# Reordering the front of a state-space and gated-FFN kernel: rate placement in portions, more result buffers, iotas before waiting loads

## The chip, the cores and the metric

The kernel runs on one core of a Trainium2 chip. A core has five engines that work side by side: TensorE (PE in the profile) multiplies matrices and writes to PSUM; VectorE (DVE) and ScalarE (ACT) do elementwise work; GpSimd (POOL) does elementwise work and issues DMAs; SyncE (SP) only issues DMAs here. Each engine takes its instructions in one fixed order, and waits for another engine by semaphores. The metric is the device time of one execution in microseconds, less is better, as the median of several runs.

## The reference

`x` is 2048 tokens of 576 channels. The output and the gradients with respect to twelve of the inputs are wanted:

```python
xn = layernorm(x)                                  # over the 576 channels
P = exp((dt * A)[:, :, None] * arange(2048))       # 576 channels, 128 states, complex
K = einsum("dn,dnl,dn->dl", C, P, dt * B).real     # a convolution kernel per channel
s = irfft(rfft(xn, 4096) * rfft(K, 4096))[:2048] + xn * Dskip
g = silu((silu(xn @ w1) * (xn @ w3)) @ w2)         # hidden width 4608
out = x + s * g
```

Matrices are bf16. The change concerns the absolute value of P, that is real exponentials exp(dt * A_re * l).

## The kernel before

The program is one long straight line of instructions in stages: a front (`prologue`, lines 314 to 486) of some 88 us; a middle stage that builds K and runs the hidden layer of the gated FFN at once (`ssm_forward`, `ffn_hidden`); the FFN's output; and a backward pass of over 1000 us.

**What the front makes.** The real exponentials are split: position l is written as a sum of a coarse and a fine part, so a channel needs 16 + 64 columns instead of 2048. For 36 chunks of 16 channels that makes 36 x 1280 columns of 128 states. `early_exps` (line 678) computes them in 45 pieces of 1024 columns, numbered 0 to 44 below. One piece takes: TensorE products of a chunk's rates (`LR_`, 80 rows: 16 channels in three bf16 parts, with gaps) with a selection matrix (`sel_base`, made from iotas), into a PSUM tile of which there are two (`e_ps`); one ScalarE exponential into an SBUF tile `E_k`, of which there are four; and one store of 256 KB from SyncE's queue to DRAM (`E_dram`). For pieces 0 to 30 each product is issued twice, with the same result (`(0, 0, 1, 1) if n < 31`, line 683).

**Placing the rates.** `place_rates` (line 656) moves the rates of some chunks from the layout of the input (channels on partitions) into the rows that the products above want. For eight chunks it issues 48 small products (128 rows, 32 columns of weights, 128 columns wide: three parts, eight chunks, two halves) into one PSUM tile `t_ps`, of which there are two, and then one VectorE copy to `LR_`. It is called for chunks 0 to 3, 4 to 11, 12 to 19, 20 to 27 and 28 to 35. A chunk has 1280 columns, so chunk c is first read by piece 1.25 c.

**The selection matrix.** `selector_values` (line 546) has GpSimd write four iotas; `selector_base` (line 566) has VectorE turn them into the two parts of `sel_base` in place: 1024 columns for the fine positions and 256 for the coarse ones.

**The layer norm.** `ln_load` loads the even token tiles and copies the odd ones to DRAM in turned order (`odd_copy`); `ln_load_odd` loads them from there on GpSimd's queue, so it waits for that copy to land. `ln_stats` (line 205) takes statistics of 16 tiles on VectorE, `ln_root` the root of the variances, `ln_scale` the scaled tiles `xn_bf`; `ln_turn` (line 240) turns them on TensorE, ten steps with a VectorE copy each into `xnT`; `ln_fold` (line 259) makes eight sums and differences of tiles on VectorE that the Fourier spectrum of xn reads.

**What sets the order.** A scheduler orders each engine's instructions by a priority that the kernel sets (`self.pre(us)`), as far as data and buffers allow. In the front the order is pinned further: `Chain` (line 77) queues every instruction that is called through it behind the one before, for VectorE (`self.V`), ScalarE (`self.S`), GpSimd (`self.G`); `in_order` (line 651) does so for TensorE's placing products, exponential products and turns; `Behind` queues a SyncE load behind a given store. Such an edge holds only between instructions of one engine, and orders their issue without a wait. The text of `prologue` is therefore the order of work: `run(n)` issues pieces until n have been issued.

Other parts that the prediction speaks of: `load_rates` loads C and B behind early stores; the eight products Wr, Wi (lines 411 to 415) run on GpSimd; `store3` stores phase rates from GpSimd; `phase_rows` (line 717) issues twelve small loads `lhs_t` on SyncE's queue; `build_selectors` and `dft_signs` are short VectorE work; `early_spectrum` (line 692) transforms xn on TensorE, with copies to `u_e` on VectorE and ScalarE; the first steps of the hidden layer run between those.

## Time and profile before

| | us |
|---|---|
| median of 3 runs | 1737.71 (1734.06 to 1741.98) |
| the profiled execution | 1742.17 |
| its span, first to last instruction | 1740.0 |
| TensorE busy in the span | 1621.5 (93%) |
| VectorE busy | 1406.1 (81%) |
| ScalarE busy | 914.6 (53%) |
| GpSimd busy | 439.2 (25%) |

The mean granted clock of TensorE was 0.978. The profile gives, for each instruction, its start within the span, its duration, its line and the tiles that it writes and reads (`out<-in`), and for idle time what ended it. Where instructions go through a `Chain` they all show line 87, and `Behind` shows line 99, so one tells them apart by their tiles. A window gives the busy time of each engine in a stretch of the span, the clock that TensorE was granted (1.00 is full), and the share of time in which the DMA engines were busy; that share can exceed 1 a little in short stretches.

### The profile page before, as it was taken

The page shows a single profiled execution, that of the slowest core. Times are in us where ns is not written, and L with a number is a line of the kernel's source. Part 1 is how long each engine was busy: PE and PEld are TensorE (multiplying, and loading weights), DVE is VectorE, ACT ScalarE, POOL GpSimd, SP SyncE. Part 2 cuts the span into 40 slices and gives each one's busy share as a digit, 9 for nine tenths or more (in the row PEclk, how much of TensorE's full clock was granted, in tenths as well). Part 3 has the DMA queues.
Part 4 walks back from the last instruction along what each step waited for, and adds up shares of the span by engine and source line. Part 5 has one row for each costly group of instructions (what it writes and reads, how often), then busy time and mean ns, then how long its engine had stood idle before and what let it go on. Part 6 is the DMA issues. An engine that isn't in the chain of part 4 may idle for free. (4 is left out here: it accounts for less than half of the span.)

```text
span 1740.0 us, 33185 instructions
## 1 busy us (share of the span) xinstructions
PE 1621.5 (93%) x12784; PEld 981.9 (56%) x12841; DVE 1406.1 (81%) x2170; ACT 914.6 (53%) x1674; POOL 439.2 (25%) x675
## 2 busy tenths in 40 slices
PE   7798999999997999989999999999999998999998
PEld 4453444444444777545555555655555576777776
DVE  6669899989891656687975999678989966899898
ACT  5667778886762112585765857574655502111111
POOL 7142333322232111012111111111121351122143
PEclk8899999999998999999999999999999999999999
DMA  6558999998789999649577684969999999999992
GB/s 204 211 209 310 306 332 322 314 312 265 246 264 190 248 218 205 206 119 276 148 222 207 190 233 142 243 173 249 208 244 224 239 235 237 224 204 212 235 203 50
DMA packets 622060, 394.87 MB, mean 227 GB/s; under 512 B 426798, under 2 KB 565678, under 8 KB 621902
## 3 DMA queue, kind: packets, MB, share of 16 engines
q1 hardware_dynamic: 560140, 252.69, 59.8%
q0 software_dynamic: 39968, 121.11, 22.4%
q10 hardware_dynamic: 21794, 18.95, 3.7%
q8 instruction: 100, 1.64, 0.4%
q14 instruction: 58, 0.48, 0.1%
HBM read 122.18 MB, written 182.13 MB: 175 GB/s over the span
## 5 line engine op out<-in xcount | busy, mean ns | idle before, releaser
L2018 PEld LDWEIGHTS <-acts 128*128 128x128 bf16 x2304 | 222.7, 98 | 63.1 <-DMA acts<-GG_dram 1.7
L1966 PE MATMUL pgw<-ggu,xn_bf 128*128 128x512 bf16 x1152 | 256.6, 382 | 0.1
L1501 DVE TENSOR_TENSOR pr_q<-et_ps,pz 128x1024 f32<-128x1024 f32 x144 | 176.1, 1223 | 27.8 <-PE et_ps L1495 18.6
L1966 PEld LDWEIGHTS <-xn_bf 128*128 128x128 bf16 x1152 | 112.3, 98 | 133.0 <-issue 4.2
L1123 PEld LDWEIGHTS <-xnT 128*128 128x128 bf16 x1152 | 107.4, 98 | 140.6 <-issue 36.7
L1505 DVE TENSOR_REDUCE S_b<-pr_q 128x64 f32<-128x1024 f32 x144 | 175.4, 1218 | 3.9
L1878 PE MATMUL ph<-w2T,goT 128*128 128x512 bf16 (+3 forms) x800 | 159.1, 367 | 9.7 <-ACT gw L1968 3.5
L1123 PE MATMUL pg<-wmB_w,xnT 128*128 128x512 bf16 x532 | 148.8, 381 | 8.1 <-issue 5.0
L1123 PE MATMUL pu<-wmB_w,xnT 128*128 128x512 bf16 x563 | 150.3, 380 | 1.5 <-ACT u_t L1143 0.6
L1944 PE MATMUL pgw<-go_o,h_n 128*128 128x288 bf16 x1152 | 150.0, 287 | 1.1 <-ACT gh L1896 0.8
L1944 PEld LDWEIGHTS <-h_n 128*128 128x128 bf16 x1152 | 111.3, 98 | 31.4 <-issue 1.0
L1138 ACT ACTIVATE s_t<-pg 128x512 bf16<-128x512 f32 x144 | 87.3, 606 | 76.2 <-PE pu L1132 33.7
L2018 PE MATMUL px<-wT_ggu,acts 128*128 128x288 bf16 x896 | 121.9, 288 | 0.9 <-DMA wT_ggu<-in_B_w_dram 0.9
L1486 ACT COPY gz<-gz 64x1024 bf16<-64x1024 bf16 x36 | 37.5, 1043 | 159.3 <-DMA gz<-gK_dram 151.6
L1878 PEld LDWEIGHTS <-goT 128*128 128x128 bf16 (+1 forms) x800 | 65.0, 99 | 94.5 <-issue 39.6
L2018 PE MATMUL px<-wA,acts 128*128 128x288 bf16 x832 | 109.8, 286 | 1.9 <-DMA acts<-GG_dram 1.4
L1949 POOL DMA_DIRECT2D out_dram<-gw x36 | 20.1, 560 | 333.6 <-ACT gw L1948 323.6
L1972 POOL DMA_DIRECT2D out_dram<-gw x72 | 51.2, 715 | 209.8 <-ACT gw L1968 182.1
L1152 POOL DMA_DIRECT2D G_dram<-g_t x72 | 51.2, 712 | 187.7 <-ACT g_t L1140 121.2
L779 ACT ACTIVATE cs_k<-et_ps 128x512 bf16<-128x512 int16 x180 | 92.6, 629 | 1.2 <-PE et_ps L777 1.1
L1143 ACT CAST u_t<-pu 128x512 bf16<-128x512 f32 x144 | 86.6, 601 | 11.6 <-PE pu L1123 9.4
L1838 DVE TENSOR_TENSOR ggu<-ggu,h_n 128x1024 bf16<-128x1024 bf16 x72 | 48.9, 686 | 43.8 <-ACT ggu L1850 43.7
(342 smaller groups left out, 3212.8 us busy)
## 6 DMA issues: line engine op xcount, KB each, us to landing
G_dram<-g_t POOLq DMA_DIRECT2D x72, 256.0 KB, 4.9
U_dram<-u_t POOLq DMA_DIRECT2D x72, 256.0 KB, 4.8
H_dram<-h_t SPq DMA_DIRECT2D x72, 256.0 KB
Q_dram<-q_k SPq DMA_DIRECT2D x36, 512.0 KB
ggu<-G_dram POOLq DMA_DIRECT2D x18, 1024.0 KB, 9.5
h_n<-U_dram POOLq DMA_DIRECT2D x18, 1024.0 KB, 9.2
GG_dram<-ggu SPq DMA_DIRECT2D x36, 512.0 KB
GU_dram<-ggu SPq DMA_DIRECT2D x36, 512.0 KB
```

Source lines behind the costliest of these rows:

```text
L779: self.sin_last = nc.scalar.activation(out=CS[:, :, o:o + 256], in_=pt[:].bitcast(I16)[:, :, 0::2], func=ACT.Sin, scale=6.283184 / 2 ** 16)
L1123: ins = nc.tensor.matmul(pt[:], lhsT=xnT[:, c, ts], rhs=wm[w][:, c, :], start=(q == 0 and c == 0), stop=(q == 1 and c == nfull - 1))
L1138: nc.scalar.activation(out=s_t[:, :, q, :], in_=pgv, func=ACT.Silu)
L1143: nc.scalar.copy(out=u_t[:, :, q, :], in_=puv)
L1152: self.u_stores[step] = nc.gpsimd.dma_start(out=dst[fb * ng:(fb + 1) * ng, i0 // 4, :, i0 % 4:i0 % 4 + NT, :].rearrange("g p t f -> p g (t ...
L1501: nc.vector.tensor_tensor(out=pr[:], in0=T[z][:].rearrange("p s k d f j -> p (s k) (d f j)")[:, None] .to_broadcast([P, 2, 4, 4 * AV]), in ...
L1505: nc.vector.tensor_reduce(out=self.sums_of[-1][:, :, :, z, :, dg, d0:d0 + 8].rearrange("p r s k d -> p (r s) k d"), in_=pr[:].rearrange("p ...
L1878: prev = nc.tensor.matmul(dst(j, k), lhsT=lw, rhs=rh, start=start, stop=stop)
L1944: self.pe_last = nc.tensor.matmul(pgw[pi_][:, 0:pw], lhsT=hn[:, tt, fl * P:(fl + 1) * P], rhs=self.go_o[:, tt, po:po + pw], start=(tt == 0 ...
L1966: self.pe_last = nc.tensor.matmul(pw_[:], lhsT=self.xn_bf[:, tt, c * P:(c + 1) * P], rhs=ggu[:, :, tt, :], start=(n == 0), stop=(n == LT - 1))
L1972: self.gp(lambda: nc.gpsimd.dma_start(out=aps[names[w]][(c - 1) * P:(c + 1) * P, fb:fb + FG].rearrange("(c p) f -> p c f", p=P), in_=gw[:, ...
L2018: self.pe_last = nc.tensor.matmul(px[pi_][:, 0:pw], lhsT=acts[i][:, ai, fi, :], rhs=w[:, po:po + pw], start=(n == 0), stop=(n == len(steps ...
```

## The change

- **Iotas first.** The odd loads are issued behind the four iotas of the selection matrix instead of ahead of the last one; GpSimd's chain now begins at the last iota.
- **The base in two parts.** The 1024-column part of `sel_base`, then the copy of the first four chunks' rates, then the 256-column part; piece 0 is issued before the placing of chunks 4 to 11.
- **Portions.** `place_rates` becomes a generator that pauses after every eight products. For chunks 12 to 19, 20 to 27 and 28 to 35 each pause issues one piece (`mixed`): pieces 4 to 9, 14 to 19 and 26 to 31.
- **Statistics.** The statistics of the even tiles come behind the placing of chunks 12 to 19, and the scaling of the odd tiles behind that of 28 to 35.
- **Four more result buffers** (`E_m`), in the space that the first spectrum tiles `u_e` use later; pieces n with n mod 8 above 3 use them.
- **Doubling.** Products are issued twice for pieces 12 to 34 only, in place of 0 to 30.
- **Turns and folds.** The ten turning steps stand before pieces 35 to 44, one each; the eight folds come behind the last turn instead of between the turns.
- **Loads.** The twelve `lhs_t` loads are queued behind the store of piece 44 instead of 34.
- **GpSimd.** `self.G.prev = self.V.prev` names an instruction of another engine, so the next GpSimd instruction of the chain (the first of Wr) has no predecessor in it.

```diff
             self.ln_load(lsb)
-            self.G.prev = self.odd_copy
-            self.ln_load_odd(self.G)
             self.pre(0.5)
             self.selector_values(st, selp)
+            self.ln_load_odd(self.G)
...
-            self.selector_base()
+            self.selector_base(0)
             LR_ = lp.tile([P, D // 16, N], BF16, name="lhs_r")
-            self.place_rates(0, 4, pc, place, LR_, tps)
-            self.place_rates(4, 12, pc, place, LR_, tps)
-            ex = self.early_exps(LR_, ep, eps)
+            for _ in self.place_rates(0, 4, pc, place, LR_, tps):
+                pass
+            self.selector_base(1)
+            more = up.tile([P, 4, 1024], BF16, name="E_m", tag="u_e")
+            ex = self.early_exps(LR_, ep, more, eps)
             run = lambda n: [next(ex) for _ in range(n - len(self.exps))]
+            def mixed(c0, c1):
+                part = self.place_rates(c0, c1, pc, place, LR_, tps)
+                for _ in part:
+                    next(ex)
+            run(1)
+            for _ in self.place_rates(4, 12, pc, place, LR_, tps):
+                pass
...
+            run(4)
+            self.pre(9)
+            mixed(12, 20)
             last = self.ln_stats(even, small)
-            run(8)
-            self.pre(9)
             self.load_rates(tmp, (1, 3, 5, 7))
-            self.place_rates(12, 20, pc, place, LR_, tps)
-            run(15)
+            run(14)
             self.pre(17)
             last = self.ln_stats(odd, small, last)
-            self.place_rates(20, 28, pc, place, LR_, tps)
+            mixed(20, 28)
             self.ln_root(small, last)
+            self.G.prev = self.V.prev
             self.ln_scale(even)
+            run(26)
+            mixed(28, 36)
             self.ln_scale(odd)
...
-            run(28)
             self.pre(38)
-            self.place_rates(28, 36, pc, place, LR_, tps)
             turns = chain(self.ln_turn(even, tps), self.ln_turn(odd, tps))
             fold = self.ln_fold()
-            for n in (31, 32, 34, 35, 36, 38, 39, 40, 42, 43):
+            for n in (35, 36, 37, 38, 39, 40, 41, 42, 43, 44):
                 run(n)
                 self.pre(40)
                 next(turns)
-                next(fold, None)
             run(45)
+            for _ in fold:
+                pass
...
-            self.lhs_0 = self.phase_rows(0, selp, "lhs_0", Behind(self.tc, nc.sync, self.e_stores[34]))
+            self.lhs_0 = self.phase_rows(0, selp, "lhs_0", Behind(self.tc, nc.sync, self.e_stores[44]))
...
+                if (c - c0) % 4 == 3:
+                    yield
...
-                E = ep.tile([P, 1024], BF16, name="E_k")
+                E = more[:, n % 4] if n % 8 > 3 else ep.tile([P, 1024], BF16, name="E_k")[:]
                 pe = ps.tile([P, 1024], FP32, name="e_ps")
-                for k in (0, 0, 1, 1) if n < 31 else (0, 1):
+                for k in (0, 0, 1, 1) if 11 < n < 35 else (0, 1):
```

More of the change, by code (lines that the diff above doesn't have):

```diff
@@ L552, in io @@
         def io(out, pattern):
-            nc.gpsimd.iota(out, pattern=pattern, base=0, channel_multiplier=0, allow_small_or_imprecise_dtypes=True)
+            return nc.gpsimd.iota(out, pattern=pattern, base=0, channel_multiplier=0, allow_small_or_imprecise_dtypes=True)
         io(dl[:], [[1, DC], [0, BV]])
@@ L557, in selector_values @@
         io(dlp[:], [[1, DC], [0, AP]])
-        io(val[:, QW:], [[0, DC], [2 * BV, 2], [4 * BV, AP // 2]])
+        self.G.prev = io(val[:, QW:], [[0, DC], [2 * BV, 2], [4 * BV, AP // 2]])
     def selector_rows(self, st):
@@ L564, in selector_rows, with selector_base @@
         self.V.tensor_copy(out=self.sel_pm[:], in_=pmi[:])
-    def selector_base(self):
+    def selector_base(self, part):
         QW = 16 * self.cfg.BV
-        for sl, dl in ((slice(0, QW), self.sel_dl), (slice(QW, QW + 8 * self.cfg.AV), self.sel_dlp)):
+        for sl, dl in ((slice(0, QW), self.sel_dl), (slice(QW, QW + 8 * self.cfg.AV), self.sel_dlp))[part:part + 1]:
             self.V.scalar_tensor_tensor(out=self.sel_base[:, sl], in0=dl[:], scalar=self.sel_pm[:, 0:1],
@@ L663, in place_rates, with early_exps @@
                                                            stop=(h == 1)))
+                if (c - c0) % 4 == 3:
+                    yield
         self.V.tensor_copy(out=LR_[0:80, c0:c1].rearrange("p c n -> p (c n)"), in_=pt[0:80, 0:(c1 - c0) * P])
-    def early_exps(self, LR_, ep, ps):
+    def early_exps(self, LR_, ep, more, ps):
         nc, cfg = self.nc, self.cfg
@@ L687, in early_exps @@
                 self.exps.append(self.e_last)
-                self.S.activation(out=E[:], in_=pe[:], func=ACT.Exp)
-                self.e_stores.append(nc.sync.dma_start(out=self.E_dram[c4 // 4, :, o:o + 1024], in_=E[:]))
+                self.S.activation(out=E, in_=pe[:], func=ACT.Exp)
+                self.e_stores.append(nc.sync.dma_start(out=self.E_dram[c4 // 4, :, o:o + 1024], in_=E))
                 yield
```

## The prediction

> **What bounds the kernel now.** I began with the time around the span: the profiled execution took 1742.17 us, its span 1740.0; the median of the runs is 1737.71. The change touches only the front, so I asked what the stages behind it are bound by, in a table of windows: busy us of each engine with its instructions, granted clock, DMA share, GB/s.
>
> ```profile
> 15.36:18.77 3.41, 1.67 (x10) 0.99 (x11) 2.81 (x4) 0.59 (x1) 3.41 (x5) 1.00 0.67 239
> 18.77:32.42 13.65, 13.51 (x66) 6.77 (x64) 9.48 (x28) 7.54 (x8) 9.21 (x11) 0.50 0.71 208
> 36.00:40.00 4.00, 3.52 (x20) 1.74 (x18) 4.00 (x17) 3.51 (x5) 3.94 (x6) 1.00 0.73 235
> 66.00:77.00 11.00, 10.05 (x101) 6.38 (x100) 8.95 (x14) 9.82 (x11) 0.00 (x0) 1.00 0.52 182
> 18.00:88.00 70.00, 59.47 (x426) 34.17 (x425) 48.13 (x117) 44.24 (x46) 28.55 (x27) 0.82 0.62 205
> 90.00:130.00 40.00, 39.04 (x228) 21.07 (x230) 24.01 (x31) 24.13 (x43) 21.36 (x21) 0.99 0.60 209
> 130.00:400.00 270.00, 251.18 (x2225) 114.18 (x2263) 247.05 (x393) 219.39 (x435) 79.05 (x118) 0.99 0.93 315
> ```
>
> From 90 on TensorE is busy 39.04 us of 40, and from 130 to 400 251.18 of 270, with DMA at 0.93: full stages, whose work starts when the front hands over. From 18 to 88 the clock averages 0.82 and TensorE's 59.47 busy us are mostly products at half clock. ScalarE's own rows (start, us, operation, and in brackets the idle time before and what ended it) show what paces the front, the 45 exponentials E_k, which I number 0 to 44.
>
> ```profile
> 10.36 1.28 ACT L87 ACT_TABLE_LOAD   x1
> ...
> 18.18 2.00 ACT L87 ACTIVATE E_k<-e_ps 128x1024 bf16<-128x1024 f32 x2 [6.54 <-PE e_ps L683]
> 21.15 1.02 ACT L87 ACTIVATE E_k<-e_ps 128x1024 bf16<-128x1024 f32 x1 [0.98 <-PE e_ps L683]
> ...
> 29.73 1.02 ACT L87 ACTIVATE E_k<-e_ps 128x1024 bf16<-128x1024 f32 x1 [0.68 <-PE e_ps L683]
> 34.36 1.94 ACT L87 ACTIVATE E_k<-e_ps 128x1024 bf16<-128x1024 f32 x2 [3.61 <-PE e_ps L683]
> ...
> 58.31 1.94 ACT L87 ACTIVATE E_k<-e_ps 128x1024 bf16<-128x1024 f32 x2 [3.37 <-DMA E_dram<-E_k]
> ...
> 65.42 1.94 ACT L87 ACTIVATE E_k<-e_ps 128x1024 bf16<-128x1024 f32 x2 [3.36 <-PE e_ps L683]
> 67.60 8.46 ACT L87 ACTIVATE E_k<-e_ps 128x1024 bf16<-128x1024 f32 x9 [0.25 <-ACT E_k L87]
> 79.95 1.94 ACT L87 ACTIVATE E_k<-e_ps 128x1024 bf16<-128x1024 f32 x2 [3.89 <-DMA E_dram<-E_k]
> ...
> 85.79 1.94 ACT L87 ACTIVATE E_k<-e_ps 128x1024 bf16<-128x1024 f32 x2 [0.94 <-PE e_ps L683]
> ```
>
> The last exponential ends at 85.79 + 1.94 = 87.73. The 45 start 18.18 us into the span although the table was ready at 11.64; from 21.15 to 29.73 they come every 1.71 us; placing bursts leave gaps of 3.61 and 3.36; twice the buffers wait for their stores (3.37, 3.89). Undisturbed, single ones come every 0.94 (nine in 8.46). Now why they start late, from the rows of all engines, and what the products cost, from TensorE's own:
>
> ```profile
> 11.02 1.28 DVE L87 SCALAR_TENSOR_TENSOR sel_val<-sel_dl,pm,sel_val 128x1024 bf16<-128x1024 bf16 x1
> 11.15 2.67 PE L661 MATMUL t_ps<-pc,place 128*32 128x128 bf16 x56 [0.78 <-DVE pc L87]
> 12.34 2.93 POOL L87 DMA_DIRECT2D xt<-odd_A_u  x4 [6.24 <-DMA odd_A_u<-in_A_u_dram]
> 15.28 0.65 POOL L553 IOTA sel_val<- 128x256 bf16 x1
> 15.96 0.48 DVE L87 SCALAR_TENSOR_TENSOR sel_val<-sel_dlp,pm,sel_val 128x256 bf16<-128x256 bf16 x1 [3.67 <-POOL sel_val L553]
> 16.36 1.81 DVE L87 CAST lhs_r<-t_ps 80x512 bf16<-80x512 f32 x2
> 17.10 12.55 PE L683 MATMUL e_ps<-sel_val,lhs_r 80*128 80x512 bf16 x38 [3.29 <-DVE lhs_r L87]
> ...
> 29.58 3.73 PE L661 MATMUL t_ps<-pc,place 128*32 128x128 bf16 x48
> 40.76 2.44 PE L661 MATMUL t_ps<-pc,place 128*32 128x128 bf16 x48
> ...
> 47.52 1.94 PE L683 MATMUL e_ps<-sel_val,lhs_r 80*128 80x512 bf16 x8 [0.24 <-ACT E_k L87]
> ```
>
> GpSimd stands 6.24 us in front of the odd loads; the small iota behind them ends at 15.93, the second base operation waits for it, and everything follows. A burst of 48 placing products takes 2.44 at full clock (51 ns each), 3.73 mostly at half. Two doubled exponentials take 1.94 of products and 0.24 of waiting, so they come every 1.09; at half clock one takes 1.71, so a single one's products are about 0.43 at full and 0.86 at half, doubled ones 0.86 at full.
>
> **Part by part.** *Iotas first.* Moving one iota of 0.65 ahead of the loads puts it inside the 6.24 us wait: the loads issue no later, and what follows in GpSimd's chain neither. If the wait were gone it would cost 0.65. The first base operation still ends at 12.30; the copy of four chunks' rates (0.60, half the 1.21 of eight; the two together are the 1.81) ends at 12.9; the first exponential reads only that base and chunk 0. Its product (0.43) and its hand-over to ScalarE (0.2, what the first one shows beyond its four products) put it at 13.6 in place of 18.18. What is late next is the second burst, now behind it: 13.4 + 2.45 = 15.9, so the second exponential starts at 16.5. The portion base (0.48) stands on VectorE before it.
>
> *Twelve undoubled.* Eleven further exponentials run at ScalarE's 0.94, whether with a portion or not: 8 placing products are 0.41, which with 0.43 leaves TensorE idle a tenth. They end the stretch at 16.5 + 11 x 0.94 = 26.9. This needs the clock, which I come to.
>
> *Portions.* The bursts go as six portions of eight: in exponentials 4 to 9 they are free; in 14 to 19 and 26 to 31, doubled, TensorE needs 0.41 + 0.86 = 1.27 for each and becomes the bound. Sum: 2 x 1.09 + 6 x 1.27 + 6 x 1.09 + 6 x 1.27 + 3 x 1.09 = 27.2, to 54.1; then ten single ones between turns, 10 x 0.94, to **63.5**. The gaps of 3.61 and 3.36 are gone; the price is 12 x 0.18 = 2.2, in the sum.
>
> *What VectorE must deliver.* Each rate copy now waits behind six exponentials, and what is queued behind it waits too: the statistics. Its rows:
>
> ```profile
> 23.56 0.76 DVE L87 BATCH_NORM_STATS2 stats<-xt 128x6 f32<-128x288 bf16 x2
> ...
> 24.35 0.76 DVE L87 BATCH_NORM_STATS2 stats<-xt 128x6 f32<-128x288 bf16 x2
> ...
> 44.82 1.11 DVE L87 TENSOR_SCALAR rt_a<-rt_v 128x16 int32<-128x16 int32 x1
> ...
> 52.79 5.53 DVE L87 TENSOR_SCALAR xn_bf<-xt,rstd,negmr 128x576 bf16<-128x576 bf16 x16
> ...
> 68.61 0.75 DVE L87 TENSOR_TENSOR xt<-xn_bf 128x1152 bf16<-128x1152 bf16 x1
> 69.28 0.68 DVE L87 COPY xnT<-t_ps 128x1024 bf16<-128x1024 bf16 x1
> ...
> 85.93 0.14 DVE L87 TENSOR_SCALAR dft_pb<-dft_pi 128x1 int32<-128x1 int32 x1
> ...
> 88.35 0.60 DVE L87 TENSOR_SCALAR SEL<-sel_val,rp,rs 128x256 bf16<-128x256 bf16 x2
> 88.86 1.42 DVE L87 CAST u_e<-t_ps 128x576 bf16<-128x576 f32 x2
> ```
>
> The third copy cannot end before about 25.4; sixteen tiles at 0.79 (from 23.56 to 24.35, two statistics and an aggregate) end at 38.3, and the copy for chunks 20 to 27 at 39.5, against 41.5 when exponential 25 wants it. The root took 8 from about 44.8 to 52.79, with 1.11 for an operation on 16 columns while GpSimd computes its weights beside it. Keeping 8.4, half the scaling (2.8) ends at 50.7, the last rate copy at 52.2 (wanted near 53.5) and the other half at 55.0, just when the turns begin. Covered, with 1 to 2 us to spare. The weights' chain loses its tie to the stores; where they go instead no row shows. Between the root's 8 us saved and as much of the margin lost, I take nothing, since the two work side by side in this row already.
>
> *Four more buffers.* A result may stay eight exponentials instead of four. The row for 36 to 40 has 0.73 x 4 us of DMA for 3.7 stores, 0.79 each. All DMA from 18 to 88 is 0.62 x 70 = 43 us; it must now fit into some 46. Eight times 1.09 is 8.7 us against the 4.4 that were overrun by 3.37, so I cost the stalls at nothing; the 3.89 stall came from the SP queue, whose rows are:
>
> ```profile
> 72.74 4.20 SPq L99 DMA_DIRECT2D lhs_t<-PCS_dram  x12
> ...
> 93.91 4.35 SPq L715 DMA_DIRECT2D UH_dram<-u_e  x4
> ```
>
> Twelve loads of 4.20 us stood ahead of finished results. Behind the last store they hold back no exponential, only the spectrum's stores, which began at 93.91, 6 us after the exponentials. Bounds for DMA: 0 to 4 us; I take 0, because the row of 0.73 is nearest.
>
> *Folds last.* Eight folds of 0.67 net (68.61 to 69.28) no longer stand between the turns' copies but behind them: from 64.5, after the last turn's copy, they end at 69.9, signs and selectors (3.0, from 85.93 to 88.95) at 72.9. Before, the first spectrum copy u_e came 1.1 after the exponentials; now 9, so 8 us late. VectorE's own copies of the hidden layer may queue there as well. TensorE has about one and a half steps of the hidden layer meanwhile (20 products of 0.21, 4.3 a step) and two spectrum groups: near 7.5. Cost between 0 and 8; I take 3. The u_e space now also waits for the last results' stores, a few us, under the same cover.
>
> *Sum.* 87.7 - 63.5 = 24, less 3: **21 us**. 1742.2 - 21 = 1721; the profiled run is 4.5 above the median, so against 1737.7 it is **1717**.
>
> **The clock.** It fell to 0.50 for the row 18.77 to 32.42, although TensorE was busy throughout. It changes on a grid of 3.41 us (from 18.77 to 32.42 are four); the step before, 15.36 to 18.77, held 1.67 busy us, all exponentials, which use 80 of 128 rows: 0.49 x 0.625 = 0.30 of the array. Doubled ones at full clock (1.94 in 2.19, so 0.49 after the latencies) kept it. At half clock, 0.625 for four steps did not bring it back; a placing burst did. With the change the thinnest stretch is exponentials 10 to 12: 0.43, 0.43 and 0.86 in 3.4 us, 0.31, if a step falls just so; by this trace's steps it holds 0.46. So I keep full clock. [...]
>
> **Rivals.**
> (a) *VectorE's tail decides*: the folds cost all 8 and DMA 4: 24 - 12 = 12, 1726. For it: VectorE's order is a chain. Against: the hidden layer's steps are ready. The same size comes from half clock in the last ten alone: 0.86 and a turn's eight transposes, as wide as placing products, at 0.82 make 1.68 for 0.94, 7.4 in ten, 21 - 7 = 14; or from one spell around exponentials 10 to 19.
> (b) *The front shrinks and the next stage does not start earlier*, because the scheduler places the hidden layer behind the spectrum or results wait for stores: gain 3, 1735. Against: the 39.04 of 40.
> (c) *Slower*: the clock falls before exponential 11 and never comes back, since no dense burst of 128-row products is left. Place: exponentials 1 to 44. Price at half clock: twelve doubled with portions (twice 0.41) at 1.71 + 0.82 = 2.53 for 1.27, 15.1; eleven doubled at 1.71 for 1.09, 6.8; ten with turns 7.4; the first eleven 4.9 (six with portions at 0.86 + 0.82, five at some 1.04): 34 us. 63.5 + 34 = 97.5, 10 late, with the folds' 3: 1751. It decides where portions at half clock (about 0.75 of the array) fall short of what brings the clock back: above 0.625, and below the 0.92 of the step to 32.42. 0.75 may well do.
> That the code does not do what it says: the iota is issued ahead of the loads and the buffers are eight by construction; only the cleared tie is open.
>
> **How the numbers follow.** Forecast (gain 16 to 26) 0.60; (a), gain 9 to 16, 0.18 (0.03 of it the last ten at half clock); (b), gain -8 to 9, 0.12; (c) 0.05; a gain over 26 (the root freed, no cost of the folds) 0.05. From these the range: 1710 to 1732, gains of 28 to 6. Under 0.5%, 8.7 us, a measurement here cannot tell from no change. Faster 0.83 (forecast, a, over 26), same 0.12, slower 0.05.
>
> **What would show it.** First exponential near 13.6, second 16.5, last one ending near 64; no store wait before E_k; clock 1.00 from 8.5 to the hidden layer; u_e near 73. Wrong would be: half clock in the front (c), TensorE idle for over 4 us behind 64 (a), or store waits.

## The result and the profile after

The changed kernel ran at a median of 1728.48 us (1716.1 to 1748.97 in 22 runs), the kernel before on the same chip at 1738.56 (1730.64 to 1756.86, 22 runs). The ratio on record is 0.9925 with a 95% interval of 0.9904 to 0.9947: a gain of 13 us, between 9 and 17; it is taken over fast runs alone, without those that took some per cent longer as a whole. The two medians lie 10 us apart. The prediction was a gain of 21, to 1717; its range of 1710 to 1732 holds the time, and the direction and most steps were right, the size was not. (Where the text on the kernel before gives other line numbers than the printed functions, the printed ones hold.)

The profiled execution of the changed kernel took 1739.13 us (span 1737.0). I read the front first. ScalarE's rows of it (start, us, operation, and in brackets the idle time before and what ended it):

```profile
13.61 1.02 ACT L87 ACTIVATE E_k<-e_ps 128x1024 bf16<-128x1024 f32 x1 [1.95 <-PE e_ps L697]
16.52 2.86 ACT L87 ACTIVATE E_k<-e_ps 128x1024 bf16<-128x1024 f32 x3 [1.89 <-PE e_ps L697]
...
27.91 1.95 ACT L87 ACTIVATE E_m<-e_ps 128x1024 bf16<-128x1024 f32 x2 [0.24 <-ACT E_k L87]
30.35 1.02 ACT L87 ACTIVATE E_m<-e_ps 128x1024 bf16<-128x1024 f32 x1 [0.50 <-PE e_ps L697]
...
66.16 1.02 ACT L87 ACTIVATE E_m<-e_ps 128x1024 bf16<-128x1024 f32 x1
```

The first exponential stands at 13.61 and the second at 16.52, as predicted; no store wait stands anywhere; the last one ends at 66.16 + 1.02 = 67.18, where 87.73 stood and 63.5 was predicted. So the exponentials gained 20.5 and not 24. TensorE's rows show which term was short, a single piece with its portion and a doubled one with its portion:

```profile
18.12 0.62 PE L673 MATMUL t_ps<-pc,place 128*32 128x128 bf16 x8
18.67 0.60 PE L697 MATMUL e_ps<-sel_val,lhs_r 80*128 80x512 bf16 x2
19.21 0.62 PE L673 MATMUL t_ps<-pc,place 128*32 128x128 bf16 x8
...
28.68 0.62 PE L673 MATMUL t_ps<-pc,place 128*32 128x128 bf16 x8
29.23 1.04 PE L697 MATMUL e_ps<-sel_val,lhs_r 80*128 80x512 bf16 x4
30.20 0.62 PE L673 MATMUL t_ps<-pc,place 128*32 128x128 bf16 x8
```

From start to start a portion is 0.55 (18.12 to 18.67), a single piece's products are 0.54, and a doubled piece's 0.97 (29.23 to 30.20). A doubled piece with a portion takes 1.52, where I had 0.41 + 0.86 = 1.27; a single one takes 1.09, where I had 0.94. VectorE's rows say whether it delivered:

```profile
38.00 1.17 DVE L87 CAST lhs_r<-t_ps 80x1024 bf16<-80x1024 f32 x1
...
40.70 1.43 DVE L87 SCALAR_TENSOR_TENSOR rt_a<-rstd 128x16 f32<-128x16 f32 x1
42.16 0.17 DVE L87 TENSOR_TENSOR rt_a<-rt_a,rt_v 128x16 f32<-128x16 f32 x1
...
50.84 2.81 DVE L87 TENSOR_SCALAR xn_bf<-xt,rstd,negmr 128x576 bf16<-128x576 bf16 x8
53.57 1.21 DVE L87 CAST lhs_r<-t_ps 80x1024 bf16<-80x1024 f32 x1
...
66.72 5.42 DVE L87 TENSOR_TENSOR xt<-xn_bf 128x1152 bf16<-128x1152 bf16 x8
...
77.14 1.41 DVE L87 CAST u_e<-t_ps 128x576 bf16<-128x576 f32 x2
```

The last two rate copies come at 38.00 and 53.57, the root takes 11.5 us (39.31 to 50.84; predicted 8.4) with 1.43 for an operation on 16 columns that elsewhere takes 0.17, the folds 5.42, and u_e comes at 77.14 (predicted 73). Last the stages, by windows (busy us of each engine with its instructions, granted clock, DMA share, GB/s); first the changed kernel, then the stages behind the first sine product before the change:

```profile
8.00:68.00 60.00, 54.28 (x486) 31.19 (x485) 51.81 (x106) 48.48 (x51) 33.47 (x34) 1.00 0.84 283
67.18:77.14 9.96, 9.48 (x44) 3.59 (x44) 9.79 (x25) 8.56 (x16) 5.11 (x4) 1.00 0.30 95
113.09:134.01 20.92, 17.59 (x141) 7.38 (x140) 16.00 (x26) 16.46 (x32) 5.87 (x9) 1.00 0.73 253
134.01:148.90 14.89, 11.58 (x34) 3.23 (x33) 12.78 (x20) 13.21 (x27) 3.14 (x6) 0.89 0.97 327
148.90:185.10 36.20, 35.56 (x377) 16.53 (x375) 30.12 (x48) 23.29 (x47) 10.72 (x16) 1.00 0.92 319
1180.00:1200.00 20.00, 5.72 (x42) 3.43 (x40) 6.73 (x6) 4.37 (x6) 1.30 (x2) 0.64 1.15 136
```

```profile
131.46:150.77 19.31, 17.38 (x138) 7.37 (x140) 16.42 (x26) 16.34 (x32) 5.91 (x9) 1.00 0.72 244
150.77:161.72 10.95, 8.76 (x27) 2.56 (x26) 10.76 (x18) 10.18 (x21) 2.53 (x4) 0.84 1.03 352
161.72:200.00 38.28, 36.24 (x376) 17.14 (x382) 32.14 (x51) 26.69 (x54) 11.26 (x17) 1.00 0.93 326
```

The clock is 1.00 through the whole front, with DMA at 0.84. The windows behind 113.09 hold nearly the same work in both kernels (552 and 541 of TensorE's products), from the first sine product of the middle stage on, and it takes 72.0 us instead of 68.5: 20.9 for 19.3 and 14.9 for 10.95, then 36.2 for 38.3. So of the lead of 20.5 at the last exponential 18.4 was left at the first sine product (131.46 - 113.09), as the tail took 2.2, and 14.9 at 200 us. The last row is from far behind the front: 5.72 busy us in 20, because of one wait.

I call lead, below, how much earlier than in the profiled kernel before TensorE's same products start (the median over all of them in a stretch, matched in order). The lead of this profile is 14.9 from 200 to 525 us and between 14.0 and 16.9 up to 1125, then falls in that one wait of 14.28 us and ends at 3.0.

### The profile page after: what moved, and what is told of

It is laid out like the page before. It is cut to its first block, busy times and chain, and to the rows that moved or that the text cites. A ratio compares the mean times of both kernels' runs of the same rounds, so it can differ in the third digit from the quotient of the medians.

```text
span 1737.0 us, 33201 instructions
## 1 busy us (share of the span) xinstructions
PE 1620.0 (93%) x12822; PEld 975.8 (56%) x12822; DVE 1408.5 (81%) x2170; ACT 914.4 (53%) x1674; POOL 439.2 (25%) x675
## 5 line engine op out<-in xcount | busy, mean ns | idle before, releaser
L1137 PE MATMUL pg<-wmB_w,xnT 128*128 128x512 bf16 x576 | 156.1, 380 | 2.3 <-DVE g_t L1156 2.1
L1982 ACT CAST gw<-pgw 128x512 bf16<-128x512 f32 x72 | 42.0, 584 | 73.8 <-PE pgw L1980 67.8
```

The source lines that it names most:

```text
L1137: ins = nc.tensor.matmul(pt[:], lhsT=xnT[:, c, ts], rhs=wm[w][:, c, :], start=(q == 0 and c == 0), stop=(q == 1 and c == nfull - 1))
```

## Experiments

Eleven more kernels and the changed one again, in three groups, each compared with the kernel before on its own chip. Where an edit is shown in part, the rest of it is said in the text. The table has where the last exponential ends, the first sine product, the lead at both and from 225 to 325 us, from the profile; and the ratio of times with its interval.

| kernel | last exp. ends | first sine product | lead there and there | lead 225 to 325 | ratio to before |
|---|---|---|---|---|---|
| as changed | 67.18 | 113.09 | 20.5, 18.4 | 14.9 | 0.9925 (0.9904 to 0.9947) |
| as changed, again | 67.18 | 113.10 | 20.5, 18.4 | 15.5 | 0.9923 (0.9892 to 0.9953) |
| no doubling | 73.78 | 119.44 | 14.0, 12.0 | 8.2 | 0.9973 (0.9939 to 1.0007) |
| bursts | 71.29 | 117.21 | 16.4, 14.3 | 10.0 | 0.9946 (0.9917 to 0.9976) |
| folds between | 70.02 | 114.12 | 17.7, 17.3 | 12.5 | 0.9941 (0.9912 to 0.9969) |
| iota late | 69.65 | 115.58 | 18.1, 15.9 | 11.9 | 0.9940 (0.9905 to 0.9974) |
| four buffers | 83.94 | 129.87 | 3.8, 1.6 | -1.4 | 1.0046 (1.0006 to 1.0086) |
| first twelve doubled | 71.43 | 117.35 | 16.3, 14.1 | 11.3 | 0.9956 (0.9925 to 0.9986) |
| portions single | 72.57 | 118.49 | 15.2, 13.0 | 9.5 | 0.9974 (0.9939 to 1.0008) |
| root free | 67.17 | 115.70 | 20.6, 15.8 | 12.6 | 0.9958 (0.9923 to 0.9993) |
| loads at 34 | 68.75 | 119.62 | 19.0, 11.8 | 11.6 | 0.9948 (0.9915 to 0.9982) |
| root and portions | 69.08 | 115.01 | 18.7, 16.5 | 14.2 | 0.9989 (0.9961 to 1.0018) |
| root, portions, loads | 70.67 | 121.17 | 17.1, 10.3 | 10.1 | 0.9984 (0.9955 to 1.0014) |

The intervals of bursts, folds between, iota late, first twelve doubled, root free and loads at 34 contain 0.9925, so the times do not tell these six from the change; what they lose is read from one profile each.

No product is doubled:

```diff
-                for k in (0, 0, 1, 1) if 11 < n < 35 else (0, 1):
+                for k in (0, 1):
```

> No product is doubled, so from piece 10 on nothing fills TensorE's rows between portions. Theory R (the clock is kept by rows: busy share times 80 of 128 rows, and falls near 0.30): single pieces at 0.94 us with 0.43 us of products hold 0.29, so the half clock comes between pieces 20 and 25 and perhaps at 10 to 13; portions there then cost 0.82 + 0.86 us and the last exponential ends at 66 to 72 us, against 67.2 in the changed kernel. [...] The time: by R the changed kernel's within 4 us either way, by G up to 5 us less, as VectorE's chain (last rate copy at 54.8) holds part of it.

Theory R held in this: half clock came, at the second of the two places that it gave, and cost more than forecast (73.78 for 66 to 72). This profile is of the longest of the ten executions, 1753 us; in the others the mean granted clock was 0.968 to 0.976, against 0.980 to 0.988 in all but one of the changed kernel's 22, so the loss of clock is not this execution's alone. The windows of this kernel, cut at its clock steps:

```profile
26.84:30.25 3.41, 2.27 (x17) 1.11 (x15) 3.41 (x13) 3.41 (x5) 2.95 (x5) 1.00 0.79 228
30.25:60.97 30.72, 29.61 (x139) 13.42 (x137) 26.88 (x65) 19.57 (x20) 18.90 (x17) 0.50 0.78 254
60.97:64.38 3.41, 3.41 (x20) 2.12 (x19) 1.89 (x5) 2.49 (x4) 0.00 (x0) 0.50 0.67 249
```

TensorE was busy 2.27 us of 3.41 in the window that lost the clock, most of it with products of 80 rows; the longest idle time in it was 0.50. So the rival G, by which the clock stays at 1.00, fell. Then half clock stayed for 34 us although TensorE was busy 29.61 us of 30.72, portions of 128 rows among it, and came back only in the window in which the turns (128 rows, 128 columns) had begun. Why in that one is open, since earlier ones were as full. That is rival (c) at work: a portion at half clock did not bring the clock back. The loss was 6.6 us, of which 1.5 are a spell of half clock from 13.18 to 16.60 (last section).

The portions go as bursts again:

```diff
                 for _ in part:
-                    next(ex)
+                    pass
+                for _ in range(6):
+                    next(ex)
```

> The three groups of 48 placing products go as bursts again, each ahead of its six pieces; all else as changed. Theory (portions are worth something, but little at full clock): portions cost 6 x 0.15 + 12 x 0.43 = 6.1 us in the changed kernel; three bursts of 2.44 leave ScalarE gaps of some 2.3 each, 6.9. If the clock stays 1.00 the last exponential ends 1 us later, at 68. If pieces 4 to 11, now single without portions (0.29 of the rows), lose the clock, the pieces after them at 1.71 instead of 1.09 add 2 to 6: 70 to 74. Rival (the portions are what the gain of the change is made of): gaps of 3.4 to 3.6 as before at each burst and half clock through to piece 20, the last exponential at 78 or later and most of the 10 to 13 us gone.

The last exponential came 4.1 later, at 71.29, by the way that the theory gave: pieces 4 to 11 without portions lost the clock (row below), and the second burst, at half clock, made a gap of 4.2; a third gap, of 2.32, was for a store.

```profile
21.99:25.40 3.41, 2.22 (x10) 0.96 (x10) 3.41 (x13) 3.41 (x5) 3.20 (x5) 1.00 0.76 255
```

```profile
36.93 1.94 ACT L87 ACTIVATE E_m<-e_ps 128x1024 bf16<-128x1024 f32 x2 [4.20 <-PE e_ps L699]
52.13 1.02 ACT L87 ACTIVATE E_k<-e_ps 128x1024 bf16<-128x1024 f32 x1 [2.32 <-DMA E_dram<-E_m]
```

So the portions are worth about 4 us, not what the rival said. That they earn it by keeping the clock rather than by hiding bursts of 2.4 us is argued and not shown apart: at full clock the expectation had bursts only 1 us behind, and no run had bursts at full clock throughout.

The folds stand between the turns again:

```diff
                 next(turns)
+                next(fold, None)
             run(45)
-            for _ in fold:
-                pass
```

> The eight folds stand between the turns' copies again. Theory T (VectorE's tail behind the exponentials is covered by the hidden layer, but for some 2 us): the last exponential ends 0 to 4 us later, since a turn waits for VectorE every 1.5 us; the first spectrum copy u_e comes at 72 to 75 in place of 77.1; the first sine product of the middle stage within 2 us of the changed kernel's 113.1; the time within 3 us of it. Rival (the tail is on the path in full): u_e 5 us earlier, first sine product 4 to 5 us earlier and the time 4 to 5 us less.

Theory T: the exponentials end 2.8 later, u_e comes 4.2 earlier (72.93), the first sine product 1.0 later. Neither place of the folds costs 8; moving them back loses 1.0 at the first sine product and 2.4 by 225 us.

The odd loads stand ahead of the iotas again:

```diff
+            self.G.prev = self.odd_copy
+            self.ln_load_odd(self.G)
             self.pre(0.5)
             self.selector_values(st, selp)
-            self.ln_load_odd(self.G)
```

> The odd loads stand ahead of the selection matrix's iotas in GpSimd's chain again (all four iotas behind them, as the chain now begins at the last one), while the base stays in two parts. Theory I (the iota edit is worth the wait of 6.2 us at GpSimd only so far as the small base part is late): the loads issue at 12.3, the small iota ends at 15.9, the second base part at 16.4; piece 0, which reads the first part alone, still starts near 13.6, piece 1 at 17 to 18 in place of 16.5, all later pieces 0.5 to 1.5 us later; the time 0 to 2 us more. Rival (the iotas carry the front's start): piece 0 at 18 and the last exponential 4 us later, the time 3 to 4 us more.

The first piece started at 13.59, the second at 17.48, the last ended at 69.65: 2.5 later, of which 1.0 is the iota and the rest a spell of half clock (18.76 to 22.17) that came with the longer gap; the theory had 0.5 to 1.5. So it is the base in two parts, with piece 0 issued ahead of the second burst, that starts piece 0 early, and the iota's place that starts the rest.

Four buffers instead of eight (the tile `E_m` is left out too):

```diff
-                E = more[:, n % 4] if n % 8 > 3 else ep.tile([P, 1024], BF16, name="E_k")[:]
+                E = ep.tile([P, 1024], BF16, name="E_k")[:]
```

> The four more result buffers are taken away; all else as changed. Theory B (the stores, 0.79 us of all queues each, fit between exponentials that come every 0.94 to 1.52 us, but an overrun needs the buffers): between pieces 4 and 34 nothing waits, or one or two waits of 1 to 3 us as before; with four buffers a result must be stored within four pieces, 3.8 us at 0.94 each, so waits come, if anywhere, in pieces 5 to 13 beside the loads and the last ten. The last exponential at 67 to 71, the time 0 to 3 us more. Rival (the buffers carry the gain): store waits of 3.4 to 3.9 as before, twice or more, the last exponential at 74 or later and half of the gain gone.

My theory fell, and the rival was right with room to spare: 16.8 us later (1.6 of it from a spell of half clock at the start, last section), and the whole gain gone. ScalarE's rows of this kernel show how:

```profile
34.59 1.94 ACT L87 ACTIVATE E_k<-e_ps 128x1024 bf16<-128x1024 f32 x2 [3.17 <-DMA E_dram<-E_k]
...
53.09 1.94 ACT L87 ACTIVATE E_k<-e_ps 128x1024 bf16<-128x1024 f32 x2 [5.06 <-DMA E_dram<-E_k]
...
58.25 1.02 ACT L87 ACTIVATE E_k<-e_ps 128x1024 bf16<-128x1024 f32 x1 [1.76 <-PE e_ps L697]
61.04 1.02 ACT L87 ACTIVATE E_k<-e_ps 128x1024 bf16<-128x1024 f32 x1 [1.76 <-PE e_ps L697]
```

```profile
51.46:54.87 3.41, 0.70 (x4) 0.29 (x3) 3.37 (x8) 1.78 (x2) 1.14 (x1) 1.00 0.43 164
54.87:75.35 20.48, 20.48 (x94) 10.64 (x93) 5.91 (x13) 9.57 (x11) 0.00 (x0) 0.50 0.35 130
```

Two store waits of 3.17 and 5.06; in the second TensorE too stood still, with 0.70 busy in a window of 3.41, and lost the clock for 20.48 us while busy throughout. A doubled piece with a portion then takes 2.79 (58.25 to 61.04); rival (c) had 2.53. The first wait, at full clock, costs less than it shows: piece 22 starts 3.4 later than in the changed kernel, 1.8 more than the 1.6 of the start. From there to the end 13.4 are lost, for the 5.06 that the second wait shows, since it took the clock too.

The first twelve pieces doubled again:

```diff
-                for k in (0, 0, 1, 1) if 11 < n < 35 else (0, 1):
+                for k in (0, 0, 1, 1) if n < 35 else (0, 1):
```

> The first twelve pieces are doubled again, to piece 34. Theory D (at full clock a doubled piece costs 1.09, with a portion 1.52, against 0.94 and 1.09 for single ones): pieces 4 to 9 give 6 x 0.43, the others 5 x 0.15, in all 3.3 us: the last exponential at 70.5, the time 2 to 3 us more. Rival (single pieces at the start put the clock at risk): the doubled start changes nothing of the clock, which is 1.00 there with or without, so all of the 3.3 is loss; if the doubled kernel is not slower, undoubling was worth nothing.

The last exponential came 4.25 later at a clock of 1.00. Piece 12 began at 31.82 instead of 27.91, 3.9 later: 0.9 by the second piece (17.39 for 16.52), 3.0 by the ten behind it. Undoubling was worth 4.25, more than the 3.3 that I had summed, which lacked the 0.9 ahead of the second piece.

Pieces with portions single:

```diff
-                for k in (0, 0, 1, 1) if 11 < n < 35 else (0, 1):
+                for k in (0, 0, 1, 1) if n in (12, 13, 20, 21, 22, 23, 24, 25, 32, 33, 34) else (0, 1):
```

> The pieces that carry a portion (14 to 19 and 26 to 31) are no longer doubled; the others stay as changed. Theory P (the portion beside a doubled piece was mis-sized: 0.55 + 0.97 = 1.52 for each, where 1.27 was taken): such a piece costs 0.55 + 0.54 = 1.09, so up to 12 x 0.43 = 5.2 us are free, the clock stays 1.00 (0.41 + 0.27 of 1.09 is 0.62 of the rows). But VectorE's copy of the last rates begins at 53.6 and piece 35 reads it, so the last exponential comes only 2 to 3 us earlier, at 64 to 65. Rival (the clock falls with single products, as where nothing was doubled): half clock from piece 14 on and the last exponential at 68 to 74.

The portions came at 1.09 as said, and piece 34 began at 53.32 instead of 56.77. But VectorE was late behind the slow root. The eight transposes of the first turn, which stand ahead of piece 35, waited each for a scaled tile (TensorE's row), and the clock fell at 54.79 in their midst; then piece 35 waited for the last rate copy, which stands behind that scaling (VectorE's row, then ScalarE's). The clock stayed at half until 68.45, in the last ten pieces: the last exponential at 72.57, 5.4 later.

```profile
53.07 2.45 PE L250 MATMUL t_ps<-ident_bf,xn_bf 128*128 128x128 bf16 x8
```

```profile
55.08 1.21 DVE L87 CAST lhs_r<-t_ps 80x1024 bf16<-80x1024 f32 x1
```

```profile
57.47 1.02 ACT L87 ACTIVATE E_k<-e_ps 128x1024 bf16<-128x1024 f32 x1 [3.13 <-PE e_ps L697]
```

Of the 5.4, 1.6 are from the start: the second exponential stood at 18.09, because the clock was at half from 13.83 to 17.25 (last section).

GpSimd's weight products wait for the last scaled odd tile:

```diff
+            self.gate_one = tmp.tile([P, 1], BF16, name="w_gate")
+            self.G.tensor_copy(out=self.gate_one[:], in_=self.xn_bf[:, odd[-1], 0:1])
             for (W, xr, xi, op) in ((Wr, self.B_re, self.B_im, ALU.subtract), (Wi, self.B_im, self.B_re, ALU.add)):
```

> GpSimd's eight weight products wait for the last scaled odd tile, so that they don't run beside VectorE's root. Theory V (the root's small operations take 1.1 to 1.4 us only because GpSimd works beside them): the root falls from 11.5 us to 3 to 5, the copy of the last rates comes at 45 to 48 instead of 53.6; the last exponential stays at 67.2 within 0.5, because TensorE's portions pace it; the time within 3 us of the changed kernel. Rival (the root is slow by itself): 11 us as before. If GpSimd's work, now beside the turns and folds, slows those, u_e comes later than 77.1 by 1 to 4 us.

```profile
39.95 0.17 DVE L87 SCALAR_TENSOR_TENSOR rt_a<-rstd 128x16 f32<-128x16 f32 x1
...
42.11 2.81 DVE L87 TENSOR_SCALAR xn_bf<-xt,rstd,negmr 128x576 bf16<-128x576 bf16 x8
52.63 1.22 DVE L87 CAST lhs_r<-t_ps 80x1024 bf16<-80x1024 f32 x1 [7.72 <-PE t_ps L675]
...
66.71 9.18 DVE L87 TENSOR_TENSOR xt<-xn_bf 128x1152 bf16<-128x1152 bf16 x8
```

Theory V held for the root: the same operations take 0.17 each, and the root 2.8 instead of 11.5. The copy of the last rates came at 52.63 and not at 45 to 48, since it now waits for the portions, and the exponentials end at 67.17, so nothing was gained there. And the folds, now beside GpSimd, took 9.18 instead of 5.42 (five of the eight kept 0.75, the three that met a product of GpSimd took 1.81 to 2.09): u_e at 79.75, first sine product 2.6 later.

The changed kernel again:

> The changed kernel unaltered, for its spread: the front repeats to the hundredth (first exponential 13.61, last ending 67.2) unless a clock step of 3.41 us falls on the thin windows at 10 to 17, which would put the last one 1.5 to 2.5 us later; the first sine product at 113 to 115; the lead over the kernel before 14 to 15 us from 200 to 500 us; behind 500 us it moves by up to 10 us either way with transfers and clock, so that only the median counts. Rival: the loss between 500 us and the end belongs to the change, and shows again at the same places (a wait of 14 us at 1182).

The front repeats to the hundredth, the lead is 15.5, and it ended at 21.9 where the first profile ended at 3.0. The wait at 1182 is not there: the same stretch in this run, the wait in the first one, and one like it in the kernel with the first twelve doubled:

```profile
1180.00:1200.00 20.00, 18.83 (x137) 9.08 (x136) 11.26 (x14) 11.63 (x18) 2.33 (x4) 1.00 1.07 246
```

```profile
1196.67 1.04 PE L1509 MATMUL et_ps<-gz,qT 64*128 64x64 bf16 x16 [14.28 <-ACT gz L1500]
```

```profile
1214.78 1.04 PE L1509 MATMUL et_ps<-gz,qT 64*128 64x64 bf16 x16 [14.29 <-ACT gz L1500]
```

So the changed kernel need not lose there. But the wait is not that one execution's alone: ten of the thirteen profiles with the change have one of over 3 us at these products, while the longest in the single profile of the kernel before is 2.01. Whether the change makes it likelier is open; the times of the runs contain it either way.

The twelve loads behind the store of piece 34 again:

```diff
-            self.lhs_0 = self.phase_rows(0, selp, "lhs_0", Behind(self.tc, nc.sync, self.e_stores[44]))
+            self.lhs_0 = self.phase_rows(0, selp, "lhs_0", Behind(self.tc, nc.sync, self.e_stores[34]))
```

> The twelve lhs_t loads stand behind the store of piece 34 again; all else as changed. Theory M (the 3.5 to 4.9 us that every kernel with the change loses between the first sine product and 200 us come from a new order of the middle stage, in which 26 sine products stand in one run instead of 18, and this edit is what made the scheduler order it so): TensorE's order there is as before the change, and the lead over the kernel before at 225 to 500 us is that at the first sine product, 17 to 18.4, within 1; the time 2 to 4 us less than the changed kernel's. Rival S (the edit was needed: 4.2 us of loads ahead of finished results on SyncE's queue hold back the exponentials): store waits at pieces 38 to 44, the last exponential 2 to 4 us later, and nothing gained. Rival N (the loss comes from what the stage finds, not from its order): the lead still falls by 3.5 or more.

Theory M held and was only half of it. The sine products stand as before the change, a run of 15 behind 3 (row of this kernel, then of the changed one), and the lead does not fall any more from the first sine product on: 11.8 and 11.6.

```profile
141.33 7.24 PE L791 MATMUL et_ps<-SEL,lhs_t 128*128 128x512 bf16 x15 [1.55 <-ACT cs_k L793]
```

```profile
136.45 11.16 PE L791 MATMUL et_ps<-SEL,lhs_t 128*128 128x512 bf16 x23 [1.63 <-ACT cs_k L793]
```

But the lead there was 11.8 instead of 18.4. The exponentials ended 1.6 later by the half clock at the start, not by stores; the rest was lost on TensorE between them and the middle stage:

```profile
78.88 1.12 PE L722 MATMUL t_ps<-xt,cCS 128*128 128x288 bf16 x4 [4.18 <-DVE u_e L87]
```

```profile
77.94 0.65 PE L722 MATMUL t_ps<-xt,cCS 128*128 128x288 bf16 x4 [0.93 <-DVE u_e L87]
```

With this edit undone the scheduler also places fewer products of the hidden layer ahead of the first spectrum copy, so TensorE waits 4.18 us for VectorE's u_e instead of 0.93, and that wait costs two windows at half clock (77.86 to 84.68). Clear of the 1.6, the edit as made is worth 14.9 - 13.2 = 1.7: it takes 3 us in the middle stage and gives nearly 5 ahead of it.

Single portions (by the edit shown above for them), and GpSimd's products behind the root:

```diff
+            self.gate_one = tmp.tile([P, 1], FP32, name="w_gate")
+            self.G.tensor_copy(out=self.gate_one[:], in_=self.negmr[:, 15:16])
             for (W, xr, xi, op) in ((Wr, self.B_re, self.B_im, ALU.subtract), (Wi, self.B_im, self.B_re, ALU.add)):
```

> Single products in the pieces with portions, and GpSimd's weight products wait for the end of the root (not, as in an earlier run, for the last scaled tile). Theory P+V (single portions failed because piece 35 then waited for the last rate copy behind the slow root; moving GpSimd's work behind the root removes that): root 3 us, last rate copy at 46 to 49, pieces 26 to 31 and 32 to 44 without a wait, the clock 1.00, the last exponential at 61 to 63 (67.2 less 12 x 0.43), folds of 5.4 as GpSimd is done by then, u_e at 71 to 73, first sine product at 108 to 110, the lead at 300 us 18 to 20 and the time 4 to 5 us less than the changed kernel's. Rival (TensorE's single products with portions lose the clock by themselves): half clock between 30 and 50 without any wait ahead of it, the last exponential at 68 or later.

```profile
42.13 10.67 DVE L87 TENSOR_SCALAR xn_bf<-xt,rstd,negmr 128x576 bf16<-128x576 bf16 x8
52.72 1.21 DVE L87 CAST lhs_r<-t_ps 80x1024 bf16<-80x1024 f32 x1
```

Missed. The root was free, but the scaling behind it took 10.67 for eight tiles instead of 2.81, so the last rate copy began at 52.72, almost as late as ever, and single portions again ended in waits for VectorE (0.90 for that copy, 1.82 for a turn's) and 6.8 us of half clock (56.90 to 63.73).

All three together:

> The kernel with single portions and the freed root, and the lhs_t loads behind the store of piece 34 besides. If both theories hold the gains add: the last exponential at 61 to 64, the first sine product at 108 to 111, the lead at 300 us 21 to 24, the time 7 to 9 us less than the changed kernel's. Rival: the loads on SyncE's queue now meet pieces that come faster (0.94 to 1.09 each from piece 14 on) and hold back pieces 40 to 44 by 2 to 4 us, so that the two together give no more than single portions and the freed root alone.

By its profile the sum of the parts' losses: the scaling, the half clock at the start, and TensorE's wait for u_e. No kernel tried beats the change. For the last two the ratios, 0.9989 and 0.9984, are also worse than their leads of 14.2 and 10.1 would give (some 0.992 and 0.994); the ratios of their medians, 0.9960 and 0.9968, less so. In their profiles the lead falls at the wait near 1190, from 13.0 to 4.3 and from 11.8 to 8.0; what the other executions lose no trace shows.

## Why the prediction was right in direction and 8 us too large

**What bounds it** held: all stages behind the front moved with it, and the lead at 225 us orders the kernels much as their times do, except for the last two.

**Iotas and base**: right to 0.1 us (13.61 and 16.52) where the clock stayed at 1.00 (18.09 for the second where it did not); the clock at 10 to 17 us was not in the working. The stretch that I named as thinnest, exponentials 10 to 12, held 2.59 busy us of 3.41 and kept the clock.

**Portions**: this is the step that failed first, as a size. "In 14 to 19 and 26 to 31, doubled, TensorE needs 0.41 + 0.86 = 1.27": it was 0.55 + 0.97 = 1.52. The row that I quoted for two doubled pieces, 1.94 of products, gives 0.97, but I used 0.86, half of the 1.71 that one takes at half clock; and 0.41 was 8/48 of a burst, without the change from one kind of product to another. By the same slip the six single pieces with portions were not free: 1.09 for 0.94, 1.0 us. For the doubled ones 12 x 0.25 is 3.0, of which the end of the stretch shows 2.6 (27.91 to 57.68 is 29.8, for 27.2). Together these are the 3.7 between 63.5 and 67.2.

**VectorE**: the copies were on time, but for the wrong reason. I kept 8.4 for the root; it was 11.5, and the last copy began at 53.57. Only because the portions were slow did nothing wait for it: with single portions the first turn and piece 35 waited for VectorE, and the clock was lost; so that the copies were on time was luck. "Between the root's 8 us saved and as much of the margin lost, I take nothing" was too kind.

**Buffers**: cost nothing with eight, as taken; with four they cost 15 us (16.8 less the 1.6). The forecast treated them as one edit among several; without them all the other edits together gain nothing (1.0046).

**Tail**: 3 taken, 2.2 measured, with u_e 4 us later than I had it. The cover that I named, the hidden layer, is there because the loads' edit reordered it; with the loads at 34 the tail took 7.1 (19.0 less 11.8), close to the 8 of rival (a). So that the 3 nearly held was luck in part.

**What was missing**: that the loads' edit changes the order of the middle stage. With the loads behind the store of 44, in ten other profiles as in the first, the lead fell by 2.3 to 4.9 from the first sine product to 225 us; in the two with 34, by 0.2. No step of the prediction had this term.

**Sum**: 24 became 20.5, the 3 became 2.2, and 3.5 were lost unforeseen: 14.9 to 15.5 in two profiles, and 13 (9 to 17) by the runs. That lies in the band that I gave to rival (a), gains of 9 to 16, and not in the forecast's 16 to 26; but (a)'s mechanism, a tail of 8 us, did not bring it.

**Clock and rival (c)**: full clock was right in both profiles of this kernel, at its start by luck (last section). The last ten pieces, single with turns, kept 1.00, so the half clock of (a) did not come; in one window there, 56.37 to 59.78 of the second profile, the products without the transposes fill 0.29 of the rows at a clock of 1.00, where every window that kept the clock had at least 0.45 with all that ran in it, transposes among it (last section). The mechanism of (c) is real: portions at half clock did not bring the clock back where it was lost (first and fifth experiment, 34 and 20.48 us at half clock). What kept it away is the doubling, the portions and the absence of waits together: the kernels without doubling, without portions and with store waits each lost the clock, for 34, 10.25 and 20.48 us. Rival (b) was wrong as put, though part of the lead is given back in the next stage.

What stays open: how the scheduler comes to these orders, and what single executions lose or win behind 500 us.

## What to carry to other kernels

Take the cost of an interleaved step from start to start in rows where the two kinds of work alternate, not from bursts of each. In the kernel with four buffers a store wait of 5.06 us left TensorE 0.70 us busy in a window of 3.41, and 20.48 us of half clock came behind it: the buffers that prevent such waits were worth as much here as all the other edits together (ratio 1.0046 without them). Look at how far an edit moves the order of the stage behind it, in the rows of that stage, before counting a lead as gain.

## What the runs showed of the hardware

**In these profiles the loss of the clock went with how little of a window of 3.41 us was filled, and the windows did not lie alike in each execution.** Spells of half clock lasted one, four, six and ten times 3.41 us (13.83 to 17.25 and 54.79 to 68.45 with single portions, 54.87 to 75.35 with four buffers, 30.25 to 64.38 without doubling). In the first profile of the changed kernel windows begin at 11.27 and 24.92, so one at 55.64; in the second one begins at 56.37. In the front of the changed kernel the thin windows kept the clock, in another kernel with the same first 12 us they did not; first the changed kernel, then the one with single portions:

```profile
11.27:14.68 3.41, 2.22 (x35) 1.62 (x34) 2.03 (x3) 1.41 (x2) 2.61 (x4) 1.00 0.69 225
24.92:28.33 3.41, 2.59 (x13) 1.13 (x12) 3.41 (x11) 3.17 (x4) 3.33 (x5) 1.00 0.74 233
```

```profile
10.42:13.83 3.41, 1.47 (x16) 0.87 (x16) 2.85 (x5) 1.47 (x2) 1.34 (x2) 1.00 0.54 188
```

With 2.22 and 2.59 busy us of 3.41 the clock stayed; with 1.47 it was lost from 13.83 to 17.25, the second burst took 4.01 instead of 2.44 us, and every later exponential came 1.6 us later (18.09 for 16.52). This happened in five of the thirteen profiles of kernels with the change, and it is a loss that the change is open to. It went with where this grid lay: eleven of these profiles are of kernels alike up to 17 us, the five that lost the clock have a step of the grid at 13.0 to 14.1, and the six that kept it have theirs at 11.3 to 12.5 and 14.7 to 15.9. Busy time alone does not order the windows: 2.27 of 3.41 lost the clock with products of 80 rows, 2.22 kept it with mostly placing products of 128. Busy time weighted by the rows that each product uses, of 128, nearly does. Of the 282 windows at full clock from about 8 to 90 us in the fourteen profiles, all 265 that kept it had 0.45 or more by this count, and 16 of the 17 that lost it 0.46 or less. The other one, of 0.65, is that in which the transposes wait one by one (single portions, to 54.79): eight that took 0.61 us together in the changed kernel are spread there over 2.45, three quarters of it counted as busy. For the way back from half clock no such level shows: windows of 0.84 stayed at half and one of 0.77 came back (no doubling).

**GpSimd beside VectorE.** In the changed kernel the root runs beside GpSimd's work, and eight of its 13 operations took 0.93 to 1.43 and five 0.17; with GpSimd's products behind the scaling (root free) all 13 took 0.17 or 0.18. A scaled tile took 1.33 in the mean beside the products instead of 0.35 (10.67 for eight in root and portions, 2.81 in the changed kernel), a fold 1.81 to 2.09 instead of 0.75 (root free). Other operations took no longer beside products: two statistics of a tile 0.76 (at 35.62 in the changed kernel), copies from PSUM in the turns 0.69 (root free, 57.16 to 64.56). What makes the difference is not shown; the longest of the root's operations, 1.32 to 1.43, are about as long as one of GpSimd's products, of which this is one of the changed kernel:

```profile
40.68 1.40 POOL L87 TENSOR_TENSOR t<-C_im_bf,B_im_bf 128x640 f32<-128x640 bf16 x1
```
